# Sending row scatters one or two at a time, each behind a one-element GpSimd copy

## The chip, the cores and the metric

The kernel runs on one core of one Trainium2 chip. A core has a matrix engine (TensorE, PE in the profile), VectorE (DVE), ScalarE (ACT), GpSimd (POOL) and SyncE (SP), each with its own queue of instructions, and 16 DMA engines that all queues share. The metric is the time of the whole kernel on the device, in microseconds. The kernel before takes 3588.42 us (median of 3 runs, 3586.74 to 3589.69).

## The reference, cut to what matters

```python
X = np.fft.fft(x, axis=1)              # x: 8 x 3072 x 256 float32
X = np.fft.fft(X, axis=2)
x = X.real.reshape(8 * 3072, 256)      # 24576 tokens of 256

do_compute = x @ w_skip > 0            # expert stage: tokens that pass are changed
e_idx = argmax(x[do_compute] @ w_gate) # one of 8 experts each, gate = its softmax weight
out = x.copy()
out[do_compute] += gate * (relu(xc @ w1[e]) @ w2[e])

return (sigmoid(out @ g_gate) * (out @ g_val)) @ g_out    # last stage, 1536 wide
```

## The kernel before, in words

There are three stages: the transforms (`fft_phase`), the experts (`moe_phase`) and the gated product (`glu_phase`). The change lies in the first.

The transform stage takes the 8 batches one after another. For each batch, `stage_a` (L265) makes the first transform in 8 pieces of 3 columns: TensorE multiplies (L275), ScalarE writes the high half `uh` (L280) and VectorE the low half `ul` (L281), and then a function `between()` is called that squeezes other work in. After that a loop runs over 13 groups g (`NG`): `stage_d` (L284) multiplies along the feature dimension, `stage_c` (L303) finishes group g - 2 (`LAG` is 2) and writes the token rows into a tile `TT` (L315, L316), one of two that alternate by batch. Each group gives two rows of tiles, `TT[:, g]` and `TT[:, 13 + g]`, with 120 tokens each.

In two halves per batch (groups 0 to 5 and 6 to 12) `gate_steps` (L329) works out for every token which expert it goes to and at what place: index tiles `idx` (three of them). Its small steps lie in a list `bg`, and `tick(budget)` runs a few of them at a time between the transforms. The last step, `scat`, adds one function per row of tiles to the list `outgoing`, 12 for the first half and 14 for the second. Each such function (`row`, L427) issues on GpSimd one indirect DMA that scatters 120 rows of 272 floats to the token's place in `yrows` in DRAM. `send(n)` (L452) takes up to n functions from the list and calls them: one after each piece of `stage_a`, and one or two after each group of the loop from g = 1 on (three in the last batch). That fixes their place in GpSimd's queue; a scatter waits for its index tile and its `TT` row. `drain()` sends all that is left at the end, after the last batch.

The order of instructions in this stage is the order in which the program writes them (`manual_schedule`), on each engine's own queue. At the start of the stage L236 copies one element of a loaded tile into a tile `held` of one element on GpSimd, so that the DMAs of the constants `gt` behind it in GpSimd's queue begin after that load. Nothing reads `held`. SP issues the loads of x (L199), those of the weights that are converted on the side (`conv_jobs`), and in the last batch but one an early read of the first tokens of expert 0 (`early`).

Of the kernel before, what the change touches and what calls it, by code (L numbers as in the profile page):

```python
# [6 lines left out]
F32 = mybir.dt.float32  # L7
# [19 lines left out]
OFF = HDR - W9  # L27
# [148 lines left out]
def fft_phase(tc, x, w_skip, w_gate, cst, yrows, counts, convs, xstack, tail, early, nb=B):  # L176
    nc = tc.nc
    px = xstack.enter_context(tc.tile_pool(name="fx", bufs=5, side="right"))
    pu = xstack.enter_context(tc.tile_pool(name="fu", bufs=1, side="right"))
    with tc.tile_pool(name="f1", bufs=1) as p1, \  # L180
# [14 lines left out]
        def load_x(b, q, parts=1):  # L195
            t = px.tile([NA, CC, D], F32, tag="x", name=f"x{b}_{q}")
            n = CC // parts
            for i in range(0, CC, n):
                nc.sync.dma_start(out=t[:, i:i + n], in_=xv[b, :, q * CC + i:q * CC + i + n, :])  # L199
            xs[b, q] = t  # L200
# [20 lines left out]
        TT = []  # L221
# [11 lines left out]
        held = p1.tile([1, 1], F32, tag="held", name="held")  # L233

        with tc.manual_schedule():
# [5 lines left out]
            def prep_d():  # L241
                nc.vector.tensor_copy(run, ebase)

                def scratch(i):
                    t = px.tile([NA, CC, D], F32, tag="x", name=f"rd_{i}")
                    return t.rearrange("p c d -> p (c d)")[:, 0:4 * HN].rearrange("p (h j n) -> p h j n", h=2, j=2)
                nf, f2 = scratch(0), scratch(1)
                for j, m in enumerate((cd, sd)):
                    for h in range(2):
                        pw = ps.tile([128, 512], F32, tag="pc", name=f"pw{j}{h}")  # L250
                        for kk in range(2):
                            nc.tensor.matmul(pw[:, 0:W9], m[:, kk, h * 128:(h + 1) * 128], w9[:, kk, :], start=kk == 0, stop=kk == 1)
                        nc.vector.tensor_copy(f2[:, h, 1 - j, 0:W9], pw[:, 0:W9])
                    nc.vector.tensor_copy(f2[:, :, 1 - j, W9:HN], m[:, :, 0:D // 2 + 1])
                nc.vector.tensor_copy(nf[:, :, 0, :], f2[:, :, 1, :])
                nc.vector.tensor_scalar_mul(nf[:, :, 1, :], f2[:, :, 0, :], -1.0)
                for j, src in enumerate((nf, f2)):
                    nc.vector.tensor_copy(rd["h", j], src)
                    nc.vector.tensor_tensor(out=rd["l", j], in0=src, in1=rd["h", j].bitcast(F32), op=ALU.subtract)
# [5 lines left out]
            def stage_a(b, between):  # L265
                uh = pu.tile([128, 2, 2, NK1, NC], F32R, tag="uh", name=f"uh{b}")
                ul = pu.tile([128, 2, 2, NK1, NC], F32R, tag="ul", name=f"ul{b}")
                U[b] = (uh, ul)
                PC = 3
                for c0 in range(0, NC, PC):  # L270
                    pa = ps.tile([128, 2, 512], F32, tag="pd", name=f"pa{b}_{c0}", bufs=3)
                    for h in range(2):
                        for ci in range(PC):
                            c = c0 + ci
                            nc.tensor.matmul(pa[:, h, ci * 2 * NK1:(ci + 1) * 2 * NK1],  # L275
                                             xs[b, c // CC][:, c % CC, h * 128:(h + 1) * 128], fa, start=True, stop=True)
                    pv = pa[:, :, 0:PC * 2 * NK1].rearrange("p h (c k) -> p h k c", c=PC)
                    oh = uh.rearrange("p h r k c -> p h (r k) c")[:, :, :, c0:c0 + PC]
                    ol = ul.rearrange("p h r k c -> p h (r k) c")[:, :, :, c0:c0 + PC]
                    nc.scalar.activation(out=oh, in_=pv, func=AF.Copy)  # L280
                    nc.vector.tensor_tensor(out=ol, in0=pv, in1=oh.bitcast(F32), op=ALU.subtract)  # L281
                    between()

            def stage_d(b, g):  # L284
                uh, ul = U[b]
                pd = ps.tile([128, 2, 512], F32, tag="pd", name=f"pd{b}_{g}", bufs=3)
                for r in range(2):
                    n = 0
                    for (u, w) in ((uh, "h"), (uh, "l"), (ul, "h")):
                        for h in range(2):  # L290
                            nc.tensor.matmul(pd[0:GR, r, 0:2 * HN],
                                             u[:, h, r, g * KS:(g + 1) * KS, :].rearrange("p k c -> p (k c)"),
                                             rd[w, r][:, h], start=n == 0, stop=n == 5)
                            n += 1
                vh = p2.tile([GR, 2, 2, HN], F32R, tag="vh", name=f"vh{b}_{g}", bufs=LAG + 1)
                vl = p2.tile([GR, 2, 2, HN], F32R, tag="vl", name=f"vl{b}_{g}", bufs=LAG + 1)
                src = pd[0:GR, :, 0:2 * HN]
                vhf = vh.rearrange("p r e n -> p r (e n)")
                nc.scalar.activation(out=vhf, in_=src, func=AF.Copy)
                nc.vector.tensor_tensor(out=vl.rearrange("p r e n -> p r (e n)"), in0=src, in1=vhf.bitcast(F32), op=ALU.subtract)  # L300
                V[b, g] = (vh, vl)

            def stage_c(b, g):  # L303
                vh, vl = V.pop((b, g))
                T = TT[b % 2]
                pc = ps.tile([128, 512], F32, tag="pc", name=f"pc{b}_{g}")
                n = 0
                for (w, v) in ((0, vh), (0, vl), (1, vh)):
                    for j in range(2):
                        rhs = v[:, :, 0, :] if j == 0 else v[:, 1::-1, 1, :]  # L310
                        nc.tensor.matmul(pc[0:GR, 0:2 * HN], gts[w][:, g, j, :], rhs, start=n == 0, stop=n == 5)
                        n += 1
                od = p2.tile([GR, HN], F32, tag="od", name=f"od{b}_{g}")
                nc.scalar.activation(out=od, in_=pc[0:GR, HN:2 * HN], func=AF.Copy)  # L314
                nc.vector.tensor_tensor(out=T[:, g, OFF:OFF + HN], in0=pc[0:GR, 0:HN], in1=od, op=ALU.add)  # L315
                nc.vector.tensor_tensor(out=T[:, NG + g, OFF:OFF + HN], in0=pc[0:GR, 0:HN], in1=od, op=ALU.subtract)  # L316
# [132 lines left out]
            outgoing = []  # L449
            cq = conv_order(convs)  # L450

            def send(n):  # L452
                while n and outgoing:
                    outgoing.pop(0)()
                    n -= 1
# [10 lines left out]
            def tick(budget, conv=True):  # L466
                credit[0] = min(credit[0] + budget, 1.3)
                while bg:
                    cost, f = bg[0]
                    if cost == STOP:  # L470
                        bg.pop(0)
                        break
                    if cost > credit[0]:
                        break
                    bg.pop(0)
                    if f:
                        f()
                    credit[0] -= cost
                while conv and cq:
                    cost, f = cq[0]  # L480
                    if cost == STOP:
                        cq.pop(0)
                        break
                    if cost > credit[0]:
                        break
                    cq.pop(0)
                    f()
                    credit[0] -= cost

            LAG = 2  # L490
            MID = 6
            for b in range(nb):
                last = b == nb - 1
                stage_a(b, lambda: (tick(.3, 0 < b < nb - 1), send(1)))
                if b == 0:
                    prep_d()
                else:
                    for g in range(NG - LAG, NG):
                        stage_c(b - 1, g)
                    bg.extend(gate_steps(b - 1, MID, NG))  # L500
                if not last:
                    for q in range(NCH):
                        load_x(b + 1, q)
                for g in range(NG):
                    stage_d(b, g)
                    if last and g:
                        tick(.8, False)
                    if g >= LAG:
                        stage_c(b, g - LAG)
                    if g - LAG + 1 == MID:  # L510
                        bg.extend(gate_steps(b, 0, MID))
                    if g:
                        tick(1.3 if last else .7, not last)
                        send(3 if last else 1 + g % 2)
            xstack.close()
            finish = tail()
            for g in range(NG - LAG, NG):
# [519 lines left out]
```

## Time and profile before

| | |
|---|---|
| median of the runs | 3588.42 us |
| profiled execution, its own time | 3595.94 us |
| its span, first to last instruction | 3594.2 us |
| mean granted TensorE clock | 0.966 of 2.4 GHz |
| TensorE busy | 3421.7 us, 95% |
| VectorE busy | 2717.8 us, 76% |
| ScalarE busy | 1758.4 us, 49% |
| GpSimd busy | 1518.4 us, 42% |

The profile is of one execution. Its page cuts the span into 40 equal slices of about 90 us and gives for each the busy share of an engine in tenths, and the clock that TensorE was granted, also in tenths (9 is 0.9 or more). The transform stage fills about the first six and a half slices. "issue" as the end of an idle time means that the engine waited for nothing that the profile shows; "remote" that it was released by something whose source isn't shown. The rest of the readings are answers of the trace to questions on a stretch, an engine or a line; they stand in the rows below.

### The profile page before, as it was taken

What the parts mean: (1) busy time and instruction counts of PE and PEld (TensorE: products, weight loads), DVE (VectorE), ACT (ScalarE), POOL (GpSimd) and SP (SyncE); (2) the same over time, 40 slices, a digit from 0 to 9 for tenths busy, and PEclk for the clock granted to TensorE, in tenths of its full rate; (3) what the DMA queues carried; (4) which work ended last, traced back from release to release, by engine and by line L of the source; (5) the groups of instructions that cost most, each with busy time, mean ns of one, the idle gap of its engine ahead of it and who ended that gap; (6) DMA issues with size and microseconds to landing.
All of it is one profiled execution on the core that took longest, in us unless ns stands there. A gap on an engine that the chain in (4) does not pass through costs nothing.

```text
span 3594.2 us, 72605 instructions
## 1 busy us (share of the span) xinstructions
PE 3421.7 (95%) x27600; PEld 3369.7 (94%) x27600; DVE 2717.8 (76%) x4546; ACT 1758.4 (49%) x4109; POOL 1518.4 (42%) x1768
## 2 busy tenths in 40 slices
PE   7878777999999899999999999999999999999999
PEld 7777777999999899999999999999999999999999
DVE  5545544444444489998999998999999899999998
ACT  3333333233332355555555555555555555555555
POOL 1343343221212354444444445444444445444444
PEclk8888878999999899999999999999999999999999
DMA  6433325223231100000000000000000000000000
GB/s 163 133 100 127 100 71 172 91 89 109 92 109 58 55 19 19 25 25 25 25 19 19 25 25 25 25 19 19 25 25 25 25 21 17 25 25 25 25 19 13
DMA packets 115950, 184.19 MB, mean 51 GB/s; under 512 B 11476, under 2 KB 91862, under 8 KB 115329
## 3 DMA queue, kind: packets, MB, share of 16 engines
q1 hardware_dynamic: 98817, 135.05, 11.9%
q0 software_dynamic: 15552, 42.97, 4.0%
q8 instruction: 230, 3.77, 0.5%
q14 instruction: 151, 1.24, 0.1%
q10 hardware_dynamic: 1200, 1.16, 0.1%
HBM read 101.79 MB, written 79.04 MB: 50 GB/s over the span
## 4 chain that ended last, share of the span: by engine, by line
PE 64%; issue 4%; DMA 2%; POOL 1%; DVE 1%; ACT 0%; POOLq 0%; SPq 0%; DVEq 0%; ACTq 0%
PE gp L860 40%; PE po L915 23%; DMA yrows<-ahead 2%; PE gpt L829 1%; POOL yrows L657 0%; POOL graw L760 0%; DVE xtl L843 0%; DMA graw<-wscr 0%; PE ph L612 0%; POOL ge L872 0%; DVE ge L884 0%; POOL ge L877 0%; DVE sg L891 0%; DMA gx<-yrows 0%; DVE ge L886 0%
## 5 line engine op out<-in xcount | busy, mean ns | idle before, releaser
L860 PE MATMUL gp<-xth,gh 128*128 128x256 f32 x4032 | 1167.1, 289 | 6.7 <-ACT gs L870 4.3
L860 PE MATMUL gp<-xth,gl 128*128 128x256 f32 x4032 | 1142.8, 283 | 2.3 <-DVE gl L810 2.3
L860 PE MATMUL gp<-xtl,gh 128*128 128x256 f32 x4032 | 1142.3, 283 | 1.3 <-DVE xtl L843 1.3
L872 POOL TENSOR_TENSOR ge<-gs 128x256 f32<-128x256 f32 x576 | 503.6, 874 | 1137.2 <-ACT gs L870 1133.3
L860 PEld LDWEIGHTS gp<-xth,gh 128*128 128x128 f32 x4032 | 773.3, 192 | 21.7 <-ACT gs L870 6.1
L897 ACT ACTIVATE hh<-sg 128x512 fp32r<-128x512 f32 x576 | 364.3, 632 | 862.5 <-DVE sg L892 862.5
L860 PEld LDWEIGHTS gp<-xth,gl 128*128 128x128 f32 x4032 | 774.0, 192 | 3.1 <-DVE gl L810 3.1
L860 PEld LDWEIGHTS gp<-xtl,gh 128*128 128x128 f32 x4032 | 774.3, 192 | 2.0 <-DVE xtl L843 2.0
L915 PE MATMUL po<-gwoh,hh 128*128 128x256 f32 x2304 | 652.5, 283 | 0.0
L915 PE MATMUL po<-gwol,hh 128*128 128x256 f32 x2304 | 652.2, 283 | 0.0
L915 PE MATMUL po<-gwoh,hl 128*128 128x256 f32 x2304 | 651.6, 283 | 0.4 <-DVE hl L902 0.4
L891 DVE TENSOR_TENSOR sg<-ge,sg 128x256 f32<-128x256 f32 x576 | 547.1, 950 | 0.0
L877 POOL TENSOR_TENSOR ge<-ge,gs 128x256 f32<-128x256 f32 x576 | 460.6, 800 | 46.4 <-ACT gs L876 1.4
L884 DVE TENSOR_TENSOR ge<-gp,ge 128x512 f32<-128x512 f32 x576 | 392.4, 681 | 107.0 <-PE gp L860 57.9
L886 DVE TENSOR_TENSOR ge<-gp,ge 128x512 f32<-128x512 f32 x576 | 398.7, 692 | 61.7 <-PE gp L860 1.4
L915 PEld LDWEIGHTS po<-gwoh,hl 128*128 128x128 f32 x2304 | 442.5, 192 | 0.8 <-DVE hl L902 0.8
L915 PEld LDWEIGHTS po<-gwoh,hh 128*128 128x128 f32 x2304 | 442.6, 192 | 0.2
L915 PEld LDWEIGHTS po<-gwol,hh 128*128 128x128 f32 x2304 | 442.6, 192 | 0.0
L902 DVE TENSOR_TENSOR hl<-sg,hh 128x512 fp32r<-128x512 f32 x576 | 395.3, 686 | 0.7 <-ACT hh L897 0.7
L432 POOL DMA_INDIRECT yrows<-TT,idx x208 | 211.3, 1016 | 352.3 <-ACT od L314 169.7
L870 ACT ACTIVATE gs<-gp 128x512 f32<-128x512 f32 x576 | 340.4, 591 | 0.4 <-PE gp L860 0.2
L843 DVE TENSOR_TENSOR xtl<-xf,xth 128x256 fp32r<-128x256 f32 x336 | 319.4, 952 | 11.1 <-ACT xth L842 11.1
(123 smaller groups left out, 5842.1 us busy)
## 6 DMA issues: line engine op xcount, KB each, us to landing
gx<-yrows SPq DMA_DIRECT2D x48, 512.0 KB
out_dram<-ob SPq DMA_DIRECT2D x47, 512.0 KB
x<-in_x_dram SPq DMA_DIRECT2D x31, 768.0 KB
ws<-in_moe_w_dram SPq DMA_DIRECT2D x16, 1024.0 KB
ahead<-yrows SPq DMA_DIRECT2D x40, 272.0 KB
yrows<-zeros SPq DMA_DIRECT2D x8, 816.0 KB
x<-yrows SPq DMA_DIRECT2D x20, 272.0 KB
wscr<-cw SPq DMA_DIRECT2D x18, 256.0 KB
```

What stands on the lines that cost most here:

```text
L432: ii = ins_of(nc.gpsimd.indirect_dma_start(out=yrows, out_offset=bass.IndirectOffsetOnAxis(ap=t["idx"][:, i:i + 1], axis=0), in_=T[:, tt, ...
L843: later.append(lambda: v.tensor_tensor(out=tl[:, a], in0=f, in1=th[:, a].bitcast(F32), op=ALU.subtract))
L860: nc.tensor.matmul(p[:, q % 2], wslice(a, wi, j), t[:, xi], start=start and n == 0, stop=n == 2, skip_group_check=True)
L870: act.activation(out=s[:, 0:2], in_=P[b, j][0], func=AF.Copy)
L872: pool.tensor_tensor(out=e[:, 0], in0=s[:, 0], in1=s[:, 1], op=ALU.add)
L877: pool.tensor_tensor(out=e[:, 1], in0=e[:, 0], in1=s[:, 2], op=ALU.subtract)
L884: v.tensor_tensor(out=e, in0=p[0], in1=e, op=ALU.subtract)
L886: v.tensor_tensor(out=e, in0=p[1], in1=e, op=ALU.add)
L891: v.tensor_tensor(out=sg[:, 1], in0=e[:, 1], in1=sg[:, 1], op=ALU.mult)
L897: act.activation(out=hh, in_=PR[b, j].rearrange("p t n -> p (t n)"), func=AF.Copy)
L902: v.tensor_tensor(out=hl, in0=PR.pop((b, j)).rearrange("p t n -> p (t n)"), in1=hh.bitcast(F32), op=ALU.subtract)
L915: nc.tensor.matmul(po[:, t], m[:, ts], w[:, j, :], start=j == 0 and n == 0 and t % 2 == 0, stop=j == NJ - 1 and n == 2, skip_group_check=True)
```

## The change

`between` and `send` get an argument: a view of one element that VectorE has just written. When rows are waiting to be sent, `send` first issues a GpSimd copy of this element into `held`, and then the scatters as before. In `stage_a` the element is of the piece of `ul` just made; in the loop over groups it is of the `TT` row that `stage_c` has just made (for g = 1 there is none yet, and no copy). `drain` sends without a copy, as before.

```diff
@@ stage_a
                     nc.vector.tensor_tensor(out=ol, in0=pv, in1=oh.bitcast(F32), op=ALU.subtract)
-                    between()
+                    between(ol.bitcast(F32)[0:1, 0, 0, 0:1])
@@ send
-            def send(n):
+            def send(n, after=None):
+                if n and outgoing and after is not None:
+                    nc.gpsimd.tensor_copy(held, after)
                 while n and outgoing:
                     outgoing.pop(0)()
                     n -= 1
@@ the loop over batches
-                stage_a(b, lambda: (tick(.3, 0 < b < nb - 1), send(1)))
+                stage_a(b, lambda made: (tick(.3, 0 < b < nb - 1), send(1, made)))
...
                     if g:
                         tick(1.3 if last else .7, not last)
-                        send(3 if last else 1 + g % 2)
+                        send(3 if last else 1 + g % 2, TT[b % 2][0:1, g - LAG, OFF:OFF + 1] if g >= LAG else None)
```

## Rows read from the trace of the kernel before

**Rows 1.** The page: two lines of the 40 slices, in tenths.
```profile
PE   7878777999999899999999999999999999999999
...
PEclk8888878999999899999999999999999999999999
```

**Rows 2.** Busy time by stretch: length, then busy us (count), clock, DMA share, GB/s.
```profile
core 0: us, PE busy (x) PEld busy (x) DVE busy (x) ACT busy (x) POOL busy (x), PEclk, DMA share, GB/s
44.00:560.00 516.00, 412.44 (x2833) 382.76 (x2831) 263.78 (x758) 183.09 (x373) 196.18 (x194) 0.82 0.34 106
186.30:253.70 67.40, 52.90 (x368) 49.63 (x367) 35.26 (x97) 23.21 (x47) 26.22 (x26) 0.82 0.33 97
```

**Rows 3.** Line L432, the scatters: duration, what ended its idle time, who waited.
```profile
L432 POOL DMA_INDIRECT yrows<-TT,idx x208: 991/1000/1490, 77.7 to 579.2; - x104
...
  issue: 87.8, 192
...
  DVE TT L315: 5.2, 5
```

**Rows 4.** GpSimd in order of time: start us, us, instruction, idle before it.
```profile
182.46 1.00 POOL L432 DMA_INDIRECT yrows<-TT,idx  x1 [19.88 <-issue]
183.76 1.00 POOL L432 DMA_INDIRECT yrows<-TT,idx  x1 [0.30 <-issue]
...
199.41 1.00 POOL L432 DMA_INDIRECT yrows<-TT,idx  x1 [0.30 <-issue]
214.65 1.25 POOL L432 DMA_INDIRECT yrows<-TT,idx  x1 [14.24 <-ACT od L314]
```

**Rows 5.** Busy time by stretch, with and without a group of scatters.
```profile
184.00:202.00 18.00, 10.35 (x69) 9.01 (x67) 6.98 (x22) 3.19 (x8) 12.75 (x13) 0.74 0.37 101
202.00:216.00 14.00, 13.53 (x93) 12.79 (x94) 9.93 (x21) 8.07 (x11) 1.25 (x1) 0.84 0.53 171
216.00:232.00 16.00, 11.67 (x85) 10.66 (x83) 5.99 (x16) 3.58 (x8) 11.35 (x11) 0.95 0.42 121
240.00:256.00 16.00, 16.00 (x124) 15.72 (x124) 11.06 (x35) 7.15 (x18) 4.32 (x5) 0.98 0.10 28
```

**Rows 6.** TensorE in order of time, inside and after two groups of scatters.
```profile
201.81 5.73 PE L275 MATMUL pa<-fa,x 128*128 128x130 f32 x27 [0.34 <-issue]
...
261.95 0.99 PE L275 MATMUL pa<-fa,x 128*128 128x130 f32 x3 [0.36 <-issue]
...
269.73 4.79 PE L275 MATMUL pa<-fa,x 128*128 128x130 f32 x20 [0.82 <-issue]
```

**Rows 7.** ScalarE in order of time, the same group as in Rows 4.
```profile
195.43 0.82 ACT L280 ACTIVATE uh<-pa 128x780 fp32r<-128x780 f32 x1 [6.13 <-issue]
...
202.70 2.04 ACT L280 ACTIVATE uh<-pa 128x780 fp32r<-128x780 f32 x2 [6.04 <-remote]
```

**Rows 8.** GpSimd in order of time, at the start of the stage.
```profile
14.11 0.18 POOL L236 COPY held<-x 1x1 f32<-1x1 f32 x1 [12.63 <-DMA x<-in_x_dram]
```

**Rows 9.** Busy time by stretch: just after a group, and at full clock.
```profile
200.00:204.00 4.00, 2.82 (x10) 2.08 (x10) 0.16 (x1) 1.30 (x2) 0.41 (x1) 0.50 0.27 57
208.00:212.00 4.00, 4.00 (x37) 4.00 (x38) 2.52 (x4) 2.44 (x3) 0.00 (x0) 1.00 0.65 211
```

**Rows 10.** Expert stage: scatters of L657 on GpSimd, then busy time by stretch.
```profile
685.38 0.98 POOL L657 DMA_INDIRECT yrows<-ahead  x1 [9.57 <-DVE ahead L655]
...
697.22 0.98 POOL L657 DMA_INDIRECT yrows<-x  x1 [9.58 <-DVE x L655]
...
680.00:700.00 20.00, 20.00 (x171) 20.00 (x170) 7.30 (x13) 5.29 (x9) 3.91 (x4) 1.00 0.11 36
```

**Rows 11.** DMA queue q8 (packets, MB, share), 182 to 204 and 234 to 250 us.
```profile
q8 instruction: 1, 0.02, 0.3%
...
q8 instruction: 1, 0.02, 0.4%
```

**Rows 12.** Waits of TensorE, 0 to 620 us: us in total, times, longest.
```profile
PE pa L275 <- issue: 32.3, 54, 1.5
```

## The prediction

> **What bounds the kernel now.** I read the page's 40 slices first, then stretches of the first stage, then single engines inside one stretch. In the slices TensorE is nine tenths busy or more nearly everywhere except in the first six or seven, and only there (and once near slice 13) does the granted clock fall to 0.7 or 0.8 [rows 1]. That is the transform stage, about 40 to 580 us, and the only place that the change touches. One batch of it lasts 67.4 us and runs 368 matmuls; over 44 to 560 us the mean granted clock is 0.82 [rows 2].
>
> The 208 scatters of L432 are written in program order between the transforms, but nothing in that order holds GpSimd back: 192 of them waited for no other engine, and sixteen, the heads of the groups, did [rows 3]. So they leave in 16 groups of 12 or 14, one every 1.30 us (182.46 to 183.76): the group that begins at 182.46 has its last, the fourteenth, at 199.41, and the next, of twelve, begins at 214.65 [rows 4]. The reader should now lay TensorE beside these groups. In 184 to 202 us it ran 69 matmuls in 18 us, in 216 to 232 us 85 in 16 us, but in 240 to 256 us, with five scatters only at its end, 124 in 16 us at clock 0.98 [rows 5]. Inside the group after these two, TensorE's own rows show what the loss is: from 261.95 to 269.73 it starts 13 matmuls (3, 3, 3, 4), each group after an idle piece with "issue" as its releaser, so no data and no other engine is waited for; 7.78 us for 13 is 1.7 per us. When the group is over, 20 follow in one piece [rows 6]. ScalarE shows the same: its evacuations in the group from 182.46 come at 195.43 and 202.70, after 6 us of idle each [rows 7]. So every engine is handed its instructions slowly while a group is moving. After it TensorE runs on at its lower level, 1.2 GHz, for some us (clock 0.50 in 200 to 204 us [rows 9]): 27 matmuls took 5.73 us from 201.81, 4.7 per us [rows 6].
>
> So the bound is TensorE, held up by the groups. At the free rate, 124/16 = 7.75 per us, the 370 matmuls that the code gives a batch (96 + 156 + 78 + 40) would take 47.7 us. A batch takes 67.4, so the 26 scatters of a batch now cost 19.7 us, 0.76 us each, low clock included.
>
> **The change part by part.**
>
> *Nothing is removed.* The same scatters go out, with the same data, 26 a batch (8 in the loop over pieces, 18 in the loop over groups).
>
> *Added:* a GpSimd copy of one element ahead of a send, 8 per batch behind L281 and 11 behind L315 (the send of g = 1 has none), while rows are waiting. The one copy of this kind in the trace took 0.18 us [rows 8]. 19 x 0.18 = 3.4 us of GpSimd per batch; with 26 x 1.30 = 33.8 it is busy 37 us of a batch, under 47.7, so GpSimd is not the bound at any pace that TensorE can reach. Cost on the path: between 0 and 19 x 0.2 = 4 us per batch if each copy were waited for; I take 0, because nobody waits for `held`.
>
> *The wait:* GpSimd's queue now stops at each copy until VectorE has made the piece. Queued behind it are scatters only. Who waits for those: VectorE's write of TT two batches later, at L315, which now waits 5.2 us in all over five times [rows 3]; the next use of an index tile, three halves later; and SP's early read of the first bins. A scatter leaves at most one half later than now (34 us), under the 100 us that three index tiles give, so I take 0 and bound it by +5 us in all. The copy also reads `ul` and TT, so VectorE's next writes there wait for it; L392 writes TT's column some 20 us after the copy's turn: 0.
>
> *Moved:* the groups dissolve into one scatter per piece (a piece is 12 matmuls; 37 in 4 us at full clock make 1.3 us [rows 9]) and one or two per step of 18 matmuls (18/7.75 = 2.3 us). This is dense: at full pace the scatters would be moving 34 of 48 us. But the loop is now closed: when the engines slow down, no next scatter leaves, and the work in hand is refilled after each instead of being run dry by twelve in a row. What a spaced scatter costs stands in no row, so from both sides:
> - Nothing: two scatters every 11.8 us in the expert stage (a pair at 685.38, the next at 697.22) leave TensorE at 171 matmuls in 20 us, fully busy, with four scatters in them [rows 10]. Then a batch takes 47.7 us.
> - The slow supply stays as it is, only cut in pieces: 33.8 us at 1.7 per us give 57 matmuls. The other 313 come at the rate of a free stretch, with what it lays by counted in: 202 to 216 us ran 93, and the next stretch ran 85 where 16 x 1.7 = 27 were supplied, so 58 had been laid by: 151/14 = 10.8 per us, a floor. 313/10.8 = 29.0, and the batch takes 62.8 us.
> - A loss: each scatter stops everything for its own 1.30 us, with nothing in hand: 47.7 + 33.8 = 81.5 us.
>
> I take a third of the way from 62.8 down to 47.7, because 10.8 is a floor and the low clock should mostly go: 57.8 us, 9.6 us less than now, 0.39 us per scatter. It holds for seven batch lengths: the first group (from 77.72) meets little, and the last 14 rows are drained without a copy. 7 x 9.6 = 67 us. What is late next is the evacuation on ScalarE and VectorE, 23 and 35 us busy in a batch [rows 2], under 57.8.
>
> *Its own time:* the profiled execution took 3595.9 us, 1.7 more than its span; 3595.9 - 67 = 3529. The runs' median is 7.5 us below the profiled one, so 3588.4 - 67 = 3521 us.
>
> **A rule beside it.** In the group from 182.46 one packet of TensorE's instruction queue moves (0.02 MB), 0.3% of 16 engines over 22 us, or 1.06 us; in 234 to 250 us, without scatters, one takes 0.4% of 16 x 16 us, 1.02 us [rows 11]. So the block itself comes no slower, and the stall is not a late block. The Trainium skill (DMA: Bandwidth & Descriptors, section Queues, rings and completion order) says that each DMA engine goes round its queues packet by packet; by that rule another queue would lose the same share to the same packets, grouped or spread, and the sum would be 0. The nearly equal 1.06 and 1.02 us agree as far as they go; the result is the third rival.
>
> **The rivals.**
> 1. *The loss goes altogether*, because it needs many scatters in a row: the 58 matmuls laid by are 7.5 us of work at 7.75 per us, which covers the first five scatters of a group. Against: at full pace the gaps are short, so little is laid by again. 7 x 19.7 = 138 us less: 3450.
> 2. *Slower: a spaced scatter costs more than a grouped one.* Place: the handing out of instructions on ScalarE and VectorE, which hand each piece on to TensorE. Now a group strikes with work laid by, about 58 matmuls; in a closed loop nothing is laid by, and each scatter holds the piece that releases the next. It decides from 0.76 us per scatter. For it: evacuations 7.3 us apart inside a group [rows 7]; TensorE in small pieces could also stay at 1.2 GHz. Against: the pairs of the expert stage [rows 10]. Price up to (81.5 - 67.4) x 7 = 99 us; at 0.9 us per scatter, 26 x 0.14 x 7 = 25 us: 3613.
> 3. *No change:* the cost goes with the bytes, 0.76 us per scatter as now: 3588. That the change doesn't hold the scatters at all is no better: L236 already holds a DMA in this way for 12.6 us [rows 8].
>
> **How the numbers follow.** The partial gain 0.45 (3490 to 3570 on its own); rival 1 0.20; rival 2 0.25; rival 3 0.10. Faster by over 0.2% (7 us, about what a measurement can tell): 0.45 + 0.20 + 0.03 of rival 3 = 0.68; within 0.2% 0.07; slower 0.25. The range runs from rival 1's 3450 to 3613, which leaves out the dearer half of rival 2 and the tip of rival 1.
>
> **What would show it.** Right: L432 spread, with a 1x1 copy ahead of one or two; a batch near 58 us; "issue" idle of TensorE at L275 well under its 32.3 us [rows 12], in pieces of under 1 us; granted clock of 44 to 560 us above 0.9; the expert stage and the last one unchanged in length. Wrong: the copies there and the batch still 67 us (rival 3), or longer with ScalarE waiting in every piece and the clock under 0.8 (rival 2), or scatters in groups as before.

## The result and the profile after

The changed kernel takes 3492.24 us (median of 4 runs, 3488.05 to 3495.70) against 3588.36 us for the kernel before on the same chip: a ratio of 0.9732 [0.9715, 0.9749], 96 us less. The profiled execution took 3495.70 us, with a span of 3493.9 us, 100.3 us less than before.

The page's slices, in tenths, where [rows 1] stand for before: the low slices in the middle of the transform stage are gone, and what is left of the fall of the clock lies in one place, at the stage's end (slices 5 and 6).
```profile
PE   7998779999998899999999999999999999999999
...
PEclk9999889999999999999999999999999999999999
```

Busy time by stretch (length, then busy us and count for each engine, clock, DMA share, GB/s), beside [rows 2]. The first row has the bounds of before, the second ends before the last batch's tail, the third is one batch, the fourth the last batch and its drain.
```profile
core 0: us, PE busy (x) PEld busy (x) DVE busy (x) ACT busy (x) POOL busy (x), PEclk, DMA share, GB/s
44.00:560.00 516.00, 451.33 (x3549) 433.25 (x3548) 314.82 (x842) 214.44 (x430) 261.67 (x353) 0.94 0.43 137
44.00:398.00 354.00, 326.15 (x2651) 315.17 (x2650) 243.31 (x690) 166.90 (x336) 192.97 (x278) 0.98 0.43 136
197.50:247.50 50.00, 45.76 (x373) 44.28 (x373) 34.91 (x100) 23.21 (x47) 31.42 (x45) 0.97 0.45 147
399.00:470.00 71.00, 40.50 (x225) 34.75 (x224) 24.45 (x79) 17.44 (x42) 48.21 (x57) 0.69 0.47 142
```
One batch, 368 matmuls in 67.40 us before [rows 2], is 373 in 50.00 us. From the first evacuation (L280) of a batch to that of the next, the lengths of the last four such stretches average 67.1 us before (66.5, 64.8, 71.8, 65.3) and 51.7 us after (49.8 to 55.5). But 399 to 470 us is as slow as anything before the change: 225 matmuls in 71 us at clock 0.69.

The scatters and their copies by line (duration min/median/max, first and last start), beside [rows 3]: there are 127 copies, and 34 of them waited for VectorE's `ul` or `TT`, 117.2 us in all; most of the others found their element ready.
```profile
L432 POOL DMA_INDIRECT yrows<-TT,idx x208: 993/1001/1547, 76.3 to 466.0; - x104
...
L454 POOL COPY held<-TT x73: 173/177/894, 88.9 to 439.3; 1x1 f32<-1x1 f32 x73
L454 POOL COPY held<-ul x54: 173/177/877, 74.5 to 383.5; 1x1 f32<-1x1 f32 x54
its engine sat idle before it (us, times) until:
  DVE ul L281: 66.3, 10
  DVE TT L315: 50.9, 24
```
GpSimd in order of time inside a batch (start, us, instruction, idle before it), beside [rows 4]: not fourteen in a row at 1.30 us, but one or two and then a copy. At 218.17 a copy waited 0.71 us for `ul`; the two at 210.07 and 211.43 didn't wait.
```profile
209.09 1.00 POOL L432 DMA_INDIRECT yrows<-TT,idx  x1 [0.30 <-DVE eq L368]
210.07 0.18 POOL L454 COPY held<-TT 1x1 f32<-1x1 f32 x1
210.43 1.00 POOL L432 DMA_INDIRECT yrows<-TT,idx  x1 [0.18 <-issue]
211.43 0.22 POOL L454 COPY held<-TT 1x1 f32<-1x1 f32 x1
212.17 1.00 POOL L432 DMA_INDIRECT yrows<-TT,idx  x1 [0.52 <-ACT od L314]
...
218.17 0.18 POOL L454 COPY held<-ul 1x1 f32<-1x1 f32 x1 [0.71 <-DVE ul L281]
218.99 1.00 POOL L432 DMA_INDIRECT yrows<-TT,idx  x1 [0.64 <-issue]
```
TensorE's waits over 0 to 620 us (us in total, times, longest), beside [rows 12]: the 32.3 us of "issue" at L275 are 2.0.
```profile
PE pc L311 <- DVE TT L316: 14.4, 8, 2.9
...
PE pa L275 <- issue: 2.0, 4, 0.8
```

*Where the time came from.* The first matmul of the expert stage starts at 450.7 us instead of 562.8 (112.1 us less). From it to the last of its kind (`ph<-th,wh` of L614, L612 before) are 656.0 us instead of 644.6 (11.4 given back), and from there to the end 2387.2 instead of 2386.8. 112.1 - 11.4 - 0.4 = 100.3 us, the difference of the spans. The three lines are of the kernel before, the changed kernel, and the changed kernel again (eighth experiment):
```profile
L612 PE MATMUL ph<-th,wh x832: 277/280/554, 562.8 to 1207.4; 128*128 128x256 f32 x167
L614 PE MATMUL ph<-th,wh x832: 277/280/564, 450.7 to 1106.7; 128*128 128x256 f32 x167
L614 PE MATMUL ph<-th,wh x832: 277/280/550, 461.0 to 1104.8; 128*128 128x256 f32 x167
```
The split at the first expert matmul belongs to one execution. In the second profile the stage starts 101.8 us earlier than before and takes 643.9 us, so nothing is given back there. What both profiles agree on is the last of these matmuls, 100.7 and 102.5 us earlier than before.

### The profile page after: what moved, and what is told of

Same layout as the page of the kernel before. It is cut to its first block, busy times and chain, and to the rows that moved or that the text cites. A ratio compares the mean times of both kernels' runs of the same rounds, so it can differ in the third digit from the quotient of the medians.

```text
span 3493.9 us, 72878 instructions
## 1 busy us (share of the span) xinstructions
PE 3368.5 (96%) x27600; PEld 3329.2 (95%) x27600; DVE 2715.8 (78%) x4546; ACT 1758.8 (50%) x4109; POOL 1548.6 (44%) x1895
## 3 DMA queue, kind: packets, MB, share of 16 engines
q0 software_dynamic: 15552, 42.97, 4.0%
## 4 chain that ended last, share of the span: by engine, by line
PE 66%; issue 4%; DMA 3%; POOL 1%; DVE 1%; ACT 0%; SPq 0%; POOLq 0%; DVEq 0%; ACTq 0%
PE gp L862 41%; PE po L917 23%; DMA yrows<-ahead 2%; PE gpt L831 1%; DMA yrows<-x 1%; POOL graw L762 0%; POOL yrows L659 0%; DVE xtl L845 0%; DVE ge L888 0%; DVE ge L886 0%; POOL ge L874 0%; DMA graw<-wscr 0%; POOL ge L879 0%; DMA gx<-yrows 0%; DVE sg L893 0%
## 5 line engine op out<-in xcount | busy, mean ns | idle before, releaser
L619 DVE SCALAR_TENSOR_TENSOR mhl<-ph,mhh 128x512 fp32r<-128x512 f32 x208 | 143.8, 691 | 246.2 <-ACT mhh L618 227.6
```

The lines of the kernel that those rows point to most:

```text
L619: nc.vector.scalar_tensor_tensor(out=b, in0=p, scalar=0.0, in1=a.bitcast(F32), op0=ALU.max, op1=ALU.subtract)
```

## The experiments

The theory: while GpSimd sends scatters back to back, the other engines are handed their instructions slowly, and the change wins because it spreads the scatters over the transforms. The rivals: the copies do it; the bytes or the queues do it; the groups need not be dissolved but only shortened. Where the kernel before is named, its median on the same chip stands beside.

**1. The copies without the tie.** The same copies at the same places, from an element that is there all along.
```diff
-                    nc.gpsimd.tensor_copy(held, after)
+                    nc.gpsimd.tensor_copy(held, fa[0:1, 0:1])
```


> The changed kernel, but the element that GpSimd copies ahead of a send is one of a constant that was loaded long before, so the copies are all there and none waits. Theory (it is the wait that spaces the scatters, so that the other engines' work in hand is refilled between them): scatters leave in groups of 12 or 14 as before, some 1.5 us apart instead of 1.3, and the time is that of before, 3570 to 3595 us. Rival (the copy itself, or the little more room between scatters, is what helps): within 15 us of the changed kernel's 3492.

3593.70 us against 3592.91, ratio 1.0002 [0.9992, 1.0011]. GpSimd in one of its groups, in order of time:
```profile
182.67 0.99 POOL L432 DMA_INDIRECT yrows<-TT,idx  x1 [18.02 <-issue]
183.97 1.00 POOL L432 DMA_INDIRECT yrows<-TT,idx  x1 [0.30 <-issue]
184.95 0.18 POOL L454 COPY held<-fa 1x1 f32<-1x1 f32 x1
185.31 1.00 POOL L432 DMA_INDIRECT yrows<-TT,idx  x1 [0.18 <-issue]
186.31 0.17 POOL L454 COPY held<-fa 1x1 f32<-1x1 f32 x1
186.66 1.00 POOL L432 DMA_INDIRECT yrows<-TT,idx  x1 [0.17 <-issue]
```
The copy fits almost wholly into the 0.30 us that lay between two scatters: they are 1.30 to 1.36 us apart, in groups as before. So the copies cost nothing that can be measured and, as instructions, bring nothing.

**2. Tied, but gathered.** The changed kernel with four rows after every fourth piece and six after every fourth group.
```diff
-  stage_a(b, lambda made: (tick(.3, 0 < b < nb - 1), send(1, made)))
+  stage_a(b, lambda made, c0: (tick(.3, 0 < b < nb - 1), send(4 if c0 % 12 == 9 else 0, made)))
...
-  send(3 if last else 1 + g % 2, TT[...] ...)
+  send(3 if last else 6 if g % 4 == 0 else 0, TT[...] ...)
```


> The changed kernel with the sends gathered: four rows after every fourth piece, six after every fourth group, each such send behind one copy; the last batch keeps its three per group. Theory (a group hurts only once the work in hand is used up, about 58 matmuls or five scatters): groups of four to six cost little, 3490 to 3510 us. Rival (every scatter beyond the first two in a row costs as much as in a group of twelve, 0.76 us): two thirds of the 26 scatters of a batch cost that again, 26 x 0.67 x 0.76 x 6 batches = 79 us, so 3560 to 3580.

3535.19 us against 3592.91, ratio 0.9840 [0.9824, 0.9856]: between the two expectations. Batches are 56 to 60 us. ScalarE in order of time beside the six scatters that start from 203.42 to 209.94 us:
```profile
207.73 0.64 ACT L299 ACTIVATE vh<-pd 120x552 fp32r<-120x552 f32 x1 [3.19 <-PE pc L311]
210.62 0.29 ACT L314 ACTIVATE od<-pc 120x138 f32<-120x138 f32 x1 [2.25 <-remote]
```
ScalarE sits idle for 3.19 and 2.25 us ahead of evacuations, and TensorE, which runs without a pause until 208.3 us, then waits 3.29 us, until 211.6, for the `od` of the second. Six in a row already cost; shortened groups gain 58 us where the change gains 96.

**3. No scatters at all.** The kernel before without them; here and in the next three the expert stage loads other rows of the same size and the last stage loads x, since the token rows are not, or not all, where they read them.
```diff
-  ii = ins_of(nc.gpsimd.indirect_dma_start(out=yrows, ..., in_=T[:, tt, :], ...))
+  pass
```


> The kernel before without the 208 scatters of the transform stage. They are left out, so the expert stage loads the cleared first rows of expert 0 each time and the last stage loads x; only the transform stage is to be read. It shows what the scatters cost there in all. Theory: a batch takes 47.7 us (the free rate) against 67.4 before and 50.4 in the changed kernel, the granted clock is over 0.97 and the idle time of TensorE put down to issue at L275 nearly goes. Rival (something else than the scatters stalls the stage, the loads of x or the conversion of weights): a batch over 58 us.

3412.63 us in one run, against 3592.91. One batch by stretch, then the three largest waits of VectorE in the kernel before that ended with "issue" (44 to 560 us: us in total, times, longest):
```profile
203.30:247.60 44.30, 43.92 (x373) 42.75 (x372) 34.07 (x98) 24.07 (x48) 0.00 (x0) 1.00 0.36 126
```
```profile
DVE vl L300 <- issue: 22.0, 9, 4.2
DVE ul L281 <- issue: 15.5, 3, 5.7
DVE TT L315 <- issue: 8.5, 7, 2.5
```
A batch is 44.4 us long, and the first matmul of the expert stage comes at 394.6. So the scatters cost 562.8 - 394.6 = 168 us of the transform stage before the change (in this kernel the expert stage has no rows to wait for, which may be a part of it), and the change takes 102 to 112 of them away. The three waits of VectorE are 46.0 us in all. Without scatters it has none of the three kinds, and TensorE has none for "issue" at L275; of ScalarE only one such wait is long before the change, the 6.13 us of [rows 7]. So TensorE and VectorE show the slow handing out of instructions plainly, ScalarE less so.

**4. Rows of 64 bytes** instead of 1088 (`in_=T[:, tt, 0:HDR]`, into a tensor of their own).

> The kernel before with rows cut to their first 16 floats: as many scatters and as many rows, in the same groups and with the same indices, 64 bytes a row instead of 1088, into a tensor of their own. The rest of the rows is left out, so the later stages are as in the run without scatters; only the transform stage is to be read. Theory A (what stalls the engines is the bytes that the scatters move to DRAM): a batch falls to 48 to 53 us. Theory B (it is the work per row: the descriptors that GpSimd writes and the DMA engines read): a batch stays at 62 to 68 us and TensorE's starts keep coming 0.7 us apart inside a group.

3581.19 us in one run, against 3592.91, with batches of 64 to 73 us.
```profile
184.00:202.00 18.00, 14.07 (x96) 12.52 (x95) 7.24 (x24) 4.79 (x11) 14.03 (x14) 0.79 0.04 7
```
In 184 to 202 us the DMA engines moved 7 GB/s (101 before [rows 5]); the clock over 44 to 560 us is 0.81 (0.82 before [rows 2]). The bytes are not the cause.

**5. Scatters of which hardly a row is written**, and **6. plain DMAs in their place.** The first keeps the 208 scatters of full rows but lowers the bound on the index, the second gives the same 120 rows of 1088 bytes to SP.
```diff
-  out=yrows, ... bounds_check=NROWS - 1, ...
+  out=heads, ... bounds_check=S // 2 - 1, ...
```
```diff
-  ii = ins_of(nc.gpsimd.indirect_dma_start(out=yrows, ..., in_=T[:, tt, :], ...))
+  nc.sync.dma_start(out=heads[k0:k0 + GR, :], in_=T[:, tt, :])
```


> The kernel before with the same 208 scatters in the same groups, but with the bound on the index lowered to 1535, so that nearly every row is dropped and nearly nothing is written, into a tensor of its own. As the rows are left out, the later stages are as in the run without scatters; only the transform stage is to be read, from the first evacuation of a batch to that of the next: 67 us before, 44.4 without scatters. Theory A (the stall comes with the row transfers on the DMA engines, small or large): a batch falls to 44 to 50 us. Theory B (it comes with GpSimd's own work on a scatter, whatever the DMA engines then do): it stays at 60 to 68 us.

> The kernel before with each scatter turned into a plain DMA that SP issues: the same 120 rows of 1088 bytes out of the same tile to DRAM, in the same groups, one row after the other instead of at indices. The scattered rows are left out, so the later stages are as in the run without scatters; only the transform stage is to be read. Theory A (many row transfers in a row hold up the engines, whoever issues them): a batch stays at 58 to 68 us. Theory B (it is GpSimd's scatters and not the rows): 44 to 50 us, as without scatters.

Both ran first on a chip on which the kernel before takes 3441.51 us (12 of its 13 runs took 3439.82 to 3444.96). There they took 3415.99 and 3420.05 us, and nothing follows, for the loss whose cause they were to find isn't there. They were run again on another chip:

> The same kernel as no_rows_pass, for a chip on which the kernel before stalls: 208 scatters in the same groups, the bound of the index at 1535, so that nearly no row is written; the later stages are as without scatters. Theory A (the row transfers on the DMA engines): a batch of 44 to 50 us. Theory B (GpSimd's own work on a scatter): 60 to 68 us.

> The same kernel as plain_rows, for a chip on which the kernel before stalls; on one where before takes some 3441 it can tell nothing. Each scatter is a plain DMA from SP of the same 120 rows of 1088 bytes; the later stages are as without scatters. Theory A (many row transfers in a row hold up the engines, whoever issues them): first evacuation of a batch to that of the next 58 to 68 us. Theory B (it is GpSimd's scatters): 44 to 50 us.

3572.47 and 3420.79 us, in one run each, against 3587.22 for the kernel before. The last four batches average 66.0 us in the first (63.5 to 70.3) and 44.4 in the second. For the first, the DMA queues over 180 to 200 us (packets, MB, share of 16 engines), and TensorE beside a group of its scatters in order of time:
```profile
q1 hardware_dynamic: 20, 0.12, 4.1%
q0 software_dynamic: 626, 0.01, 2.0%
q8 instruction: 1, 0.02, 0.5%
```
```profile
185.32 0.46 PE L275 MATMUL pa<-fa,x 128*128 128x130 f32 x2 [0.46 <-issue]
186.74 0.49 PE L275 MATMUL pa<-fa,x 128*128 128x130 f32 x2 [0.95 <-issue]
188.15 1.09 PE L275 MATMUL pa<-fa,x 128*128 128x130 f32 x4 [0.92 <-issue]
...
194.57 0.57 PE L275 MATMUL pa<-fa,x 128*128 128x130 f32 x1 [1.03 <-issue]
195.98 0.38 PE L275 MATMUL pa<-fa,x 128*128 128x130 f32 x1 [0.84 <-issue]
196.70 1.08 PE L275 MATMUL pa<-fa,x 128*128 128x130 f32 x3 [0.34 <-issue]
```
For the second, one batch and the stage by stretch:
```profile
203.30:247.60 44.30, 43.93 (x372) 42.88 (x371) 34.04 (x99) 24.10 (x48) 0.00 (x0) 1.00 0.63 208
44.00:390.00 346.00, 336.50 (x2815) 328.04 (x2814) 258.72 (x749) 181.05 (x364) 0.00 (x0) 0.99 0.49 157
```
With the DMA engines nearly empty (7 GB/s) the stall is there, almost whole: pieces of one to four matmuls, "issue" ahead of each. With the same rows moved by SP, and the DMA engines half busy, it is gone. So the loss comes with GpSimd's scatters, and not with the rows on their way. What in a scatter brings it is not shown: the scatters of the first kernel still put as many packets on q0 as those of the kernel before (15552 in either whole run), only tiny ones here (626 with 0.01 MB), and a plain DMA issued by GpSimd was not tried.

**7. The rest of the last batch spread as well.** The changed kernel with `send(1 + g % 2, ...)` in the last batch too, instead of three.

> The changed kernel with one or two rows per group in the last batch too, where it sends three. Theory (the last batch, whose scatters stand back to back from 391.6 to 446 us in the changed kernel's trace and whose granted clock is 0.69, is what kept it above a paced one): that batch becomes some 15 us shorter, and 12 rows more are drained at its end, which gives 5 to 10 us back: 3475 to 3490 us. Rival (the drained rows cost at the start of the expert stage what they cost now): 3492 or up to 10 us more.

On the chip without the loss: 3446.62 us against 3441.51, ratio 1.0016 [1.0006, 1.0026]. One batch there:
```profile
203.80:248.10 44.30, 43.92 (x373) 42.75 (x372) 34.21 (x97) 24.05 (x48) 30.95 (x46) 1.00 0.63 201
```
Scatters at the pace of the transforms, and TensorE as in the kernel without any. There it brings nothing. Repeated on a chip with the loss:

> The same kernel as last_1_2, for a chip on which the kernel before stalls: the changed kernel with one or two rows per group in the last batch too, not three. Theory (the last batch, with its scatters back to back, is where the changed kernel still stalls): 3470 to 3485 us, a ratio of 0.967 to 0.972 against 0.9724 for the changed kernel. Rival (the rows then drained at the end hold up the expert stage instead): 0.972 to 0.980.

3511.05 us against 3593.89, ratio 0.9770 [0.9754, 0.9786]: no better than the change. Two stretches of it:
```profile
399.00:436.00 37.00, 29.78 (x230) 27.89 (x228) 21.13 (x81) 13.94 (x36) 21.75 (x31) 0.90 0.36 106
...
436.00:451.00 15.00, 2.30 (x10) 1.66 (x8) 4.53 (x14) 2.88 (x7) 11.65 (x12) 0.50 0.50 155
```
The last batch is quicker (230 matmuls in 399 to 436 us, where the two profiles of the changed kernel have 143 and 147), but the rows that it leaves over are drained back to back from about 430 us to 478, and the expert stage begins beside them: from its first matmul (455.7 us) to the last of its kind (1120.8) are 665.1 us, 9.1 and 21.2 more than in the two profiles of the changed kernel.

**8. The changed kernel again.**

> The changed kernel, unchanged. In the last four runs the kernel before took 3441.5 us on their chip (number 11), against 3592.9 on the chip of the four ahead of them (number 14), and with scatters at full pace a batch took 44.4 us there, as without scatters. Theory (the slow handing out of instructions under scatters is there on some chips only, and the change saves nothing but that): where before takes some 3590, the ratio is 0.973 again; where it takes some 3441, the ratio is 1.000 to 1.003. Rival (the change saves something of its own): below 0.998 on either chip.

3488.39 us against 3587.22, ratio 0.9724 [0.9708, 0.9740], with batches of 49.5 to 56.9 us. The gain repeats where the loss is; the changed kernel itself was not run on the chip without the loss, only its variant above.

**9. Distance without a tie.** The kernel before, with two copies that wait for nothing ahead of every scatter. (An earlier form, with a GpSimd product of two 120x120 tiles ahead of each scatter, gave no time.)
```diff
                 while n and outgoing:
+                    nc.gpsimd.tensor_copy(held, fa[0:1, 0:1])
+                    nc.gpsimd.tensor_copy(held, fa[0:1, 0:1])
                     outgoing.pop(0)()
```


> The kernel before with two GpSimd copies of a constant's element ahead of each scatter and no wait: scatters 2.0 us apart (1.3 and twice the 0.35 that a copy takes between scatters in copy_no_wait), as sparse as the mean of the changed kernel (26 in 50 us), but in groups of 12 or 14 that nothing ties to the transforms. Only for a chip on which before takes some 3590. Theory (the tie is what helps, since no scatter leaves while the engines are behind): part of the gain at most, 3540 to 3590 us. Rival (the distance is what helps): 3485 to 3515.

3544.94 us against 3593.89, ratio 0.9863 [0.9847, 0.9880]. The time is that of the theory that only the tie helps, yet the trace speaks for the distance. GpSimd in order of time, then a batch and the end of the stage by stretch:
```profile
192.44 1.00 POOL L432 DMA_INDIRECT yrows<-TT,idx  x1 [0.73 <-DVE vl L300]
193.46 0.28 POOL L454 COPY held<-fa 1x1 f32<-1x1 f32 x1
193.79 0.27 POOL L455 COPY held<-fa 1x1 f32<-1x1 f32 x1
194.60 1.00 POOL L432 DMA_INDIRECT yrows<-TT,idx  x1 [0.54 <-issue]
```
```profile
205.50:249.90 44.40, 44.03 (x376) 42.85 (x374) 34.51 (x98) 24.14 (x49) 29.63 (x64) 1.00 0.58 186
403.00:530.00 127.00, 37.29 (x239) 34.33 (x238) 26.13 (x72) 18.62 (x40) 79.43 (x169) 0.61 0.38 111
```
At 2.1 us from scatter to scatter, one after the other without an end, a batch takes 44.4 us: nothing is lost. But 26 x 2.1 = 55 us of scatters don't fit into 44.4 us, so a backlog grows. The next two batches already take 51.9 and 57.8 us, and VectorE's writes of `TT` wait 19.5 us in them, three times, for the DMAs of scatters that read it. The rest is paid at the end: 239 matmuls in 127 us, while GpSimd sends what is left. That is why the time is no better than that. The theory that the tie itself matters fell here; the tie gives distance and leaves no backlog.

## Why the prediction came out as it did

The forecast was 3521 us, 67 less than before; 3492 were measured, 96 less. The mechanism held, and one term of the sum was too dear.

- *The bound and its cause* (groups of scatters slow the supply of instructions to the engines): held, on a chip that has the loss. Without scatters a batch is 44.4 us, and with the change TensorE's "issue" at L275 fell from 32.3 us to 2.0, no piece over 0.8. "Every engine" was more than its rows showed; VectorE's 46.0 us (third experiment) bear it out, ScalarE's one long wait hardly. (Of the sixteen waits read as the heads of groups, one lies inside a group, 0.3 us, and the head at 182.46 is put down to "issue"; nothing hangs on it.) One word of it was wrong: not "while a group is moving", for the stall stays when nearly no row moves and goes when SP moves them all.
- *The copies at 0*: held (1.0002 in the first experiment), and no wait of another engine is put down to L454.
- *The spaced scatter, a third of the way from 62.8 to 47.7 us*: this term was mis-sized. It came out at 51.7 us and not 57.8, and the end that it was taken from was too high: the free rate was read from 240 to 256 us, which held five scatters [rows 5], as 7.75 per us; free of them it is 373/44.3 = 8.42. By the measured free batch a scatter costs (67.1 - 44.4)/26 = 0.87 us before and (51.7 - 44.4)/26 = 0.28 after, where 0.76 and 0.39 had been forecast. So two thirds of a batch's loss went and not half: 15.4 us a batch, and seven of them make 108 us (the stage got 112 and 102 us shorter in the two profiles). The other end was no better founded: 62.8 us rests on 10.8 matmuls per us as "a floor", and a whole free batch runs 8.42. With 8.42 that end would be 33.8 + 313/8.42 = 71.0 us, more than the 67.4 of before. The third of the way was a choice, so that it came as near as 6 us a batch is in part luck.
- *What is left*: a batch still loses 7 us, and the tie doesn't keep all scatters apart. In the changed kernel's trace five in a row start 1.30 to 1.45 us apart (238.00 to 243.40), ScalarE's next evacuation comes after 4.46 us of idle at 245.17, and TensorE waits 2.66 us for `TT` at 247.13. The 14.4 us of such waits at L311 above are eight, about one a batch; they are some 2 of the 7 us, and the rest was not split up.
- *Rival 1 (many in a row are needed)* was half right: work laid by does cover a few, and seven at a mean of 1.45 us (207.79 to 216.47) pass with no pause of TensorE; six at 1.30 didn't. *Rival 2 (slower)* put a spaced scatter above 0.76 us; it costs 0.28.
- *Rival 3 (the cost goes with the bytes, grouped or spread)* fell with the result, and twice more, with 64-byte rows (3581.19 against 3592.91) and with hardly any written (3572.47 against 3587.22), where the loss stayed. The rule of the Trainium skill weighed for it (DMA: Bandwidth & Descriptors, section Queues, rings and completion order), a round by packets over the queues, does not tell this loss: with 2.0% of the DMA time in the scatters' queue a batch still takes 66.0 us.
- *The expert stage unchanged*: missed by 11.4 us in the first profile, held in the second (643.9 us against 644.6). The last batch sends three rows after each step; from 391.59 they run mostly 1.30 us apart, and the rest is drained until 466 us, beside the first expert matmuls. The stage's first 50 us hold 255 matmuls, against 334 before; 79 fewer at 214 in 25 us are 9.2 us. But in the second profile the last scatters run 17 us into the stage as well (461.0 to 478), as they did before the change (562.8 to 580), and its first 50 us hold 345. So the 11.4 us are no fixed price of the change; why the two profiles differ was not settled. Spreading the last batch as well did not help (seventh experiment).
- *Clock above 0.9 in 44 to 560 us*: held, 0.94. Up to 398 us it is 0.98.

## What to carry to other kernels

When several engines pause together with "issue" as the only cause, lay the long-running instructions of the engine that isn't paused beside the pauses; here it was GpSimd's scatters, and not their bytes. In this kernel they are best spread over the work that makes their data, and tied to it: distance alone (2.1 us) removes the stall too, but a fixed distance that is longer than the work allows is paid back as a backlog. The stage's tail, where the last rows have no work to be spread over, keeps its loss (clock 0.69 above). And where a gain is split between stages, take a second profile of the same kernel before a part of it is called a cost.

## What the runs showed that was not expected

- The loss is not the same on every chip. The kernel before takes 3587 to 3594 us on three chips and 3441.51 us on a fourth, where scatters at full pace leave a batch at 44.4 us; there a variant of the change saved nothing (1.0016). A scatter keeps GpSimd busy as long on either chip: its median is 0.999 us in the fifth experiment's first run and 1.001 in its repeat.
- Inside a group, pieces of TensorE's work start at multiples of about 0.71 us from each other: 185.32, 186.74, 188.15 and 194.57, 195.98, 196.70 above, 1.42, 1.41, 1.41 and 0.72 us apart. What keeps this beat, by what path GpSimd's scatters slow the supply of instructions to the other engines, and why one chip doesn't show it, was not settled.
